# Induced attention and a squared-ReLU feed-forward: from lanes of 480 tokens to lanes of 512

## The chip, the core and the metric

One core of one Trainium2 chip runs the whole program. The metric is the time of one execution on the device, in microseconds (us). A core has TensorE (PE in the profile; its weight loads are PEld), VectorE (DVE), ScalarE (ACT), GpSimd (POOL) and SyncE (SP), which here issues nearly all DMA transfers. Each engine works through its own instructions in the order in which the program lists them, and semaphores hold it back until its operands are there.

## The reference

Four batches of 12480 tokens of 128 channels; 32 inducing vectors attend to each batch, and the batch attends to the result. A feed-forward layer of width 2048 follows on all 49920 tokens.

```python
def mab(q, kv):
    s = scale * (q @ kv.transpose(0, 2, 1))
    s = s - s.max(-1, keepdims=True)
    a = np.exp(s)
    a /= a.sum(-1, keepdims=True) + 1e-09
    return a @ kv
h = mab(I, x)
x = mab(x, h).reshape(49920, 128)

h = np.maximum(x @ w_in, 0.0)
return h * h @ w_out
```

Everything is float32.

## The kernel before

**Lanes, groups and blocks.** A lane is 480 tokens (NR = 15 rows of S = 32). Four lanes make a group, with the 32 inducing vectors of each lane on 32 of the 128 partitions. A batch has six groups of four lanes and a seventh of two. One lane is one block of the feed-forward layer, so there are 104 blocks.

**First attention** (`First`, L412, for batches 1 to 3; `FirstBatch`, L571, for batch 0). x is loaded a group at a time, turned so that channels lie on partitions (DVE turns 32x32 blocks at L452 and SP moves them at L462; batch 0 uses PE at L711), and multiplied with the inducing vectors (L481, four narrow fp32 products with 32 columns of the array each). The maximum of each lane is taken (L488). To have one maximum over the four lanes, DVE spreads the maxima into four columns (L492), PE adds up over partitions with the matrix `same` (L495), which writes into free columns of the same PSUM bank (480 to 483 of 512), and DVE takes the maximum (L499, L506). ACT takes the exponentials (L516), DVE turns them (L526), and PE mixes the tokens (L534, 15 steps). At the end of a batch, `first_end` (L758) normalises and joins the lanes to `hT`; then the product of h and w_in is made (`wide`, L793, four fp32 products of 512 columns a batch), rounded to fp32r by ACT (L797), and the remainder taken by DVE (L802). The result `hw` holds high and low parts and serves as the first weights of the batch.

**Second attention** (`Second`, L820): scores against `hT` (L836), softmax on DVE and ACT (L842 to L870), split into a high and a low fp32r part (L873, L877), and spread by SP to `st`, four transfers a lane (L883). The lanes of the short group are read as four lanes of 256 tokens that overlap, and the two blocks put together from them.

**Feed-forward** (`ffn_block`, L964): a block has four quads of four slices of the hidden width. A quad has four first products, `hw` with `st` in fp32r (L991); ReLU on ACT in two halves (L998); the square on ACT (L1013); rounding to fp32r on DVE (`hi`, L1018) and the remainder (`lo`, L1023); and three second products a slice: hi with wo_hi, hi with wo_lo, lo with wo_hi (L1077). In the last quad of a block the fourth slice is left unsplit and takes one fp32 product instead (`exact`, L1067, weights `wo_whole`). The first two blocks of all are wholly fp32 (`PLAIN`, L1034), as the split weights aren't ready then. DVE turns the output (L1098), and SP stores it (L1105).

**Weights** arrive as 64-bit words of which both halves are read, and are decoded by one ACT and five DVE instructions per 512 columns (`weights`, L283 to L327; joined at L369 and L388).

**The order** of every engine's instructions is written out by a planner before the program runs (`Plan`, L44). Each task has engines, an assumed duration in ns, a due time and predecessors; buffers have a number of places (`room`). `run` (L84) lists the tasks one after the other: for each engine, among those that can start, the one with the earliest due time. Due times come from the start of the block (BLOCK apart, from T_MAIN on) and the constants at L195 to L217. `narrow` (L1141) puts the parts of first and second attention that fall into a group's slot (mixing of the group before, scores, second attention's scores) into one stretch on PE, as a change between narrow and wide products costs PE time in the planner (L54, L67).

```python
narrow(due, parts, ...)                       # L1177: all parts of the slot in one task
t = add("DVE", 100, lanes, due + TOP_DUE, [t])                    # L556
t = add("PE", 110, gather, due + TOP_DUE, [t], reads=[bank_])     # L557
t = add("DVE", 100, most, due + TOP_DUE, [t], reads=[bank_])      # L558
exact = j == NQ - 1 and WHOLE(b, g, k) and not plain              # L980
```

Of the kernel before, what the change touches and what calls it, by code (L numbers as in the profile page):

```python
# [22 lines left out]
NR = 15  # L23
# [3 lines left out]
class Task:  # L27
    def __init__(self, engine, ns, fn, due, needs, port, mode, takes, late, order):
# [4 lines left out]
        self.waiting = 0  # L33
        self.then = []
# [9 lines left out]
class Plan:  # L44
# [12 lines left out]
    def __init__(self, room, begin, stick=0.0, patience=(0.0, 0.0, 40.0), waits={}, margin=0.0):  # L57

        self.room, self.begin, self.stick, self.tasks = room, begin, stick, []
        self.patience = patience
        self.waits, self.margin = waits, margin
# [20 lines left out]
    def run(self):  # L84
# [15 lines left out]
        for t in self.tasks:  # L100
            t.waiting = len(set(t.needs))
            for n in set(t.needs):
                n.then.append(t)
        for t in self.tasks:
            if not t.waiting:
                offer(t)

        def room_at(t):
            at = 0.0
            n = {}  # L110
            for b in t.takes:
# [3 lines left out]
                if i >= 0:  # L115
                    for u in (old[i].users if i < len(old) else ()):
                        if u.end is None:
# [4 lines left out]
        while len(done) < len(self.tasks):  # L122
            best = None
            for e in self.ENGINES:
                pick = None
                ways = []
                for t in open_[e]:
# [6 lines left out]
                    due = t.due - self.stick if e == "PE" and mode and t.mode and free[e] > self.begin else t.due  # L134
                    ways.append((start, due, t.order, t))
                if ways:
# [4 lines left out]
                    if e in self.waits and now > self.begin:  # L141
                        over = [w for w in ways if w[1] < f[1] - self.margin and f[0] < w[0] < f[0] + ns
                                and w[0] - f[0] < self.waits[e] * (f[0] + ns - w[0])]
# [5 lines left out]
            if best is None:  # L149
                raise RuntimeError("the plan is stuck")  # L150
# [22 lines left out]
def induced_attention_then_squared_relu_ffn(  # L173
# [15 lines left out]
    lanes_of = [Q] * (N // (Q * LANE)) + ([N % (Q * LANE) // LANE] if N % (Q * LANE) else [])  # L189
    NG = len(lanes_of)  # L190
    first_lane = [sum(lanes_of[:g]) for g in range(NG)]
    groups = [(b, g) for b in range(B) for g in range(NG)]
    scale = 1.0 / math.sqrt(C)

    GB, HB, LB, MB, STB, XTB, XNB, XBB = 3, 2, 2, 2, 6, 7, 2, 2  # L195
    T_MAIN, BLOCK = 41600.0, 10300.0
    ORDER = "x0 x1 x2 x3 i0 x4 x5 x6 i1 i2 i3 o0 o1 o2 o3".split()
    W_DUE = [20500.0, 27300.0, 31000.0, 32500.0, 43500.0, 42700.0, 47000.0, 53600.0]
    FIRST_DUE, FIRST_STEP, MIX_DUE, MIX_STEP, MINI_DUE = 5800.0, 3100.0, 22400.0, 200.0, -1000.0
    SLOT, SLOT_LAST, NARROW = 20300.0, -18700.0, 880.0  # L200
    AFTER = None
    WAIT_PE, WAIT_ACT, WAIT_DVE, MARGIN = 0.0, 0.9, 0.75, 10100.0
    LOAD_LEAD, TOP_DUE, GAIN_DUE, END_DUE = 29200.0, 6000.0, 3500.0, 23100.0
    S2_LEAD_0, S2_STEP, S1_LEAD, S1_STEP = 22200.0, 1400.0, 8700.0, 5600.0
    WHOLE = lambda b, g, k: True
# [5 lines left out]
    KEPT = 5  # L211
    SPLIT_DUE, SPLIT_STEP, PLAIN_DUE = 65000.0, 200.0, 6000.0
    FIRST_PAIRS, LAST_PAIRS = 2, 1
    G1_DUE, SQ_DUE, HI_DUE, LO_DUE, OP_DUE = -3000.0, 8100.0, 3100.0, 5000.0, 14500.0
    OT_DUE = 7300.0
# [4 lines left out]
    xn_pool = ctx.enter_context(tc.tile_pool(name="xn", bufs=XNB))  # L220
    xb_pool = ctx.enter_context(tc.tile_pool(name="xb", bufs=XBB))
# [9 lines left out]
    plan = Plan(dict(xn=XNB, early=5, tp=2, s=4, xb=XBB, xt=XTB, st=STB, m=MB, h=2, o0=1, o1=1, g=GB, hi=HB, lo=LB, sw=1, a=1, d=2, e=2, et=2), T_MAIN, patience=PATIENCE,  # L231
                waits={"PE": WAIT_PE, "ACT": WAIT_ACT, "DVE": WAIT_DVE}, margin=MARGIN)
# [8 lines left out]
    ind_sb = const.tile([M, C], F32, name="ind_sb")  # L241
# [12 lines left out]
    identr = const.tile([P, P], F32R, name="identr")  # L254
# [962 lines left out]
```

## Time and profile before

| | |
|---|---|
| median of 3 runs | 1621.41 us (1621.02 to 1621.56) |
| the profiled execution's own time | 1622.28 us |
| its span on the core | 1620.2 us |
| mean granted TensorE clock | 0.995 |
| busy: DVE, ACT | 1539.8 us, 1523.3 us |
| first products of the first block begin | 51.12 us |

The page gives busy times and shares of the span, 40 slices of the span in tenths, the chain of work that ended last (followed back from the last instruction, at each step to what released it) and groups of instructions by line and form: count, busy us, mean ns of one, idle time ahead of them and what ended it. A mean duration of a matmul includes its way through the array, which overlaps with the next one; how fast they follow each other is read from runs in the chain or from the starts in the timeline.

### The profile page before, as it was taken

Reading aid. Unit: us, or ns where it says so; the run is one execution under the profiler, and the core shown is the slowest. Engines: PE = TensorE matmul, PEld = TensorE weight load, DVE = VectorE, ACT = ScalarE, POOL = GpSimd, SP = SyncE. Lnnn points to the kernel's source line nnn. Section 1 sums busy time; section 2 is a strip of 40 time slices with the busy share of each in tenths; the row PEclk is TensorE's granted clock in tenths of the full one; section 3 lists DMA queues with packets and bytes.
Section 4 is the critical chain, followed back from the end, with each engine's and each line's share of the span. In section 5 each row is a group of like instructions: output and inputs, shape, how many; then the busy total and the mean of one; then the engine's idle time right before and its main releaser. Section 6 shows DMA issues by size and latency. Waiting matters only on the chain.

```text
span 1620.2 us, 22156 instructions
## 1 busy us (share of the span) xinstructions
PE 1599.4 (99%) x8006; PEld 1285.4 (79%) x8006; DVE 1539.8 (95%) x1471; ACT 1523.3 (94%) x1423; POOL 49.8 (3%) x39
## 2 busy tenths in 40 slices
PE   7899999999999999999999999999999999999998
PEld 5478888887778888888777888888878888888886
DVE  6789999999999999999999999999999999999997
ACT  5799999999999999999999999999999999999997
POOL 0000000000000000000000000000000000000000
PEclk9899999999999999999999999999999999999999
DMA  6431322422332233233332322422312211212211
GB/s 237 121 88 36 54 68 58 92 52 59 85 63 55 56 74 68 60 70 68 80 73 45 64 64 57 91 54 58 76 34 44 43 30 29 40 29 34 43 31 19
DMA packets 249308, 101.29 MB, mean 63 GB/s; under 512 B 219088, under 2 KB 245360, under 8 KB 249200
## 3 DMA queue, kind: packets, MB, share of 16 engines
q1 hardware_dynamic: 248240, 99.77, 27.7%
q8 instruction: 63, 1.03, 0.3%
q14 instruction: 45, 0.37, 0.1%
q10 hardware_dynamic: 960, 0.11, 0.0%
HBM read 29.77 MB, written 25.56 MB: 34 GB/s over the span
## 4 chain that ended last, share of the span: by engine, by line
PE 93%; DVE 3%; DMA 2%; issue 1%; ACT 1%; SPq 0%; DVEq 0%
PE op L1077 60%; PE h L991 22%; PE op L1067 5%; PE op L1034 2%; PE na L836 1%; PE nb L534 1%; DVE lo L1023 1%; PE sp L481 1%; DMA lo_i<-in_moe_w_in_dram 1%; PE wp L793 1%; DVE hi L1018 1%; DMA xn<-in_x_dram 1%; ACT g L998 0%; PE sp L495 0%; DVE et L642 0%
## 5 line engine op out<-in xcount | busy, mean ns | idle before, releaser
L1023 DVE TENSOR_TENSOR lo<-g,hi 128x1920 fp32r<-128x1920 f32 (+1 forms) x409 | 824.3, 2016 | 24.0 <-PE op L1077 5.1
L998 ACT ACTIVATE g<-h 128x960 f32<-128x960 f32 x832 | 779.5, 979 | 48.8 <-PE h L991 33.1
L1013 ACT ACTIVATE g<-g 128x1920 f32<-128x1920 f32 (+1 forms) x419 | 757.4, 1809 | 3.4
L991 PE MATMUL h<-st,hw 128*128 128x480 f32 x1664 | 521.8, 397 | 1.3 <-ACT g L998 1.3
L1018 DVE CAST hi<-g 128x1920 fp32r<-128x1920 f32 (+1 forms) x409 | 442.0, 1081 | 15.5 <-ACT g L1013 12.3
L1077 PE MATMUL op<-hi,wo_hi 128*128 128x480 f32 x1530 | 443.6, 396 | 0.0
L1077 PE MATMUL op<-lo,wo_hi 128*128 128x480 f32 x1530 | 434.2, 381 | 0.6 <-DVE lo L1023 0.5
L1077 PE MATMUL op<-hi,wo_lo 128*128 128x480 f32 x1530 | 415.6, 380 | 0.0
L991 PEld LDWEIGHTS h<-st,hw 128*128 128x128 f32 x1664 | 309.6, 188 | 93.5 <-issue 25.6
L1077 PEld LDWEIGHTS op<-hi,wo_hi 128*128 128x128 f32 x1530 | 285.8, 188 | 70.0 <-issue 25.2
L1077 PEld LDWEIGHTS op<-lo,wo_hi 128*128 128x128 f32 x1530 | 286.3, 188 | 51.2 <-DVE lo L1023 3.3
L1077 PEld LDWEIGHTS op<-hi,wo_lo 128*128 128x128 f32 x1530 | 286.7, 188 | 47.4 <-issue 0.8
L1067 PE MATMUL op<-g,wo_whole 128*128 128x480 f32 x204 | 98.9, 566 | 0.0
L860 POOL TENSOR_SCALAR z<-z 128x15 f32<-128x15 f32 (+1 forms) x28 | 48.7, 1739 | 1497.3 <-DVE z L856 1497.3
L1098 DVE STREAM_TRANSPOSE ob<-op 128x480 f32<-128x480 f32 (+1 forms) x105 | 70.4, 671 | 2.2 <-PE op L1077 1.9
L452 DVE STREAM_TRANSPOSE xb<-xn 128x960 f32<-128x960 f32 (+1 forms) x42 | 49.2, 1171 | 9.4 <-DMA xt<-xb 8.6
L1067 PEld LDWEIGHTS op<-g,wo_whole 128*128 128x128 f32 x204 | 38.2, 188 | 8.1 <-issue 2.4
L836 PE MATMUL na<-xt,hT 128*32 128x480 f32 (+1 forms) x224 | 29.7, 559 | 0.0
L481 PE MATMUL sp<-xt,indT 128*32 128x480 f32 x156 | 23.6, 570 | 0.0
L534 PE MATMUL nb<-xn,et 128*32 128x128 f32 (+1 forms) x630 | 22.5, 275 | 0.0
L534 PEld LDWEIGHTS nb<-xn,et 128*32 128x32 f32 (+1 forms) x630 | 16.9, 109 | 7.0 <-issue 5.7
L842 DVE STREAM_TRANSPOSE d<-na 128x480 f32<-128x480 f32 (+1 forms) x28 | 18.0, 641 | 3.0 <-PE na L836 3.0
(136 smaller groups left out, 471.1 us busy)
## 6 DMA issues: line engine op xcount, KB each, us to landing
out_dram<-ob SPq DMA_DIRECT2D x412, 60.0 KB, 2.2
xn<-in_x_dram SPq DMA_DIRECT2D x24, 960.0 KB, 5.5
st<-sw SPq DMA_DIRECT2D x380, 60.0 KB, 2.0
xt<-xb SPq DMA_DIRECT2D x312, 60.0 KB, 2.0
xn<-in_x_dram SPq DMA_DIRECT2D x4, 480.0 KB, 5.5
hi_i<-in_moe_w_in_dram SPq DMA_DIRECT2D x2, 512.0 KB, 14.7
lo_i<-in_moe_w_in_dram SPq DMA_DIRECT2D x2, 512.0 KB, 17.6
hi_o<-in_moe_w_out_dram SPq DMA_DIRECT2D x2, 512.0 KB, 5.0
```

The lines of the kernel that those rows point to most:

```text
L452: nc.vector.transpose(v["xb"][:R].rearrange("p j r t -> p r j t"), self.xn[:R, :, 2 * h * S:2 * (h + 1) * S].rearrange("p r (j c) -> p r j ...
L534: nc.tensor.matmul(v["nb"][c * M:(c + 1) * M, :], self.et[:R, r, :], self.xn[:R, r, :], start=r < Q, stop=r >= NR - Q,)
L836: nc.tensor.matmul(v["na"][i * M:(i + 1) * M, :W], s["hT"][:, :M], cols[:, c:c + W], start=True, stop=True,)
L860: E.tensor_scalar(v["z"], v["z"], 1e-9, 0.0, ALU.add, ALU.add)
L991: nc.tensor.matmul(c["hp"][:, l, :LANE], s["hw"][:, f * P:(f + 1) * P], second.st[k], start=True, stop=True,)
L998: nc.scalar.activation(v["g"][:, 2 * i:2 * i + 2, :], c["hp"][:, :, :LANE], AF.Relu)
L1013: nc.scalar.activation(v["g"][:, h], v["g"][:, h], AF.Square)
L1018: nc.vector.tensor_copy(v["hi"][:, h], v["g"][:, h])
L1023: nc.vector.tensor_sub(v["lo"][:, h], v["g"][:, h], v["hi"][:, h])
L1067: nc.tensor.matmul(w["op"][:, :LANE], wo_whole, v["g"][:, 3, :], start=False, stop=False)
L1077: nc.tensor.matmul(w["op"][:, :LANE], pools["wo"][wo][:, 4 * j + l, :], v[name][:, l, :], start=(j == x_ == 0 and l == 0), stop=(j == NQ - ...
L1098: nc.vector.transpose(w["ob"][:, rows].rearrange("p r c -> p (r c)"), w["op"][:, rows.start * S:rows.stop * S])
```

## The change

- **Lanes of 512.** NR is 16. A batch has six whole groups and 192 tokens left over, which form a seventh, small group of two lanes of 96 tokens in first attention and one lane of 192 in second. T_MAIN, BLOCK and the other constants of the planner are new.
- **A shared block.** The 192 tokens left over of batches 0 and 1 make one block of 384 tokens at the end of batch 0, those of 2 and 3 one at the end of batch 2. Its first products come in two halves, each with the weights of its batch. There are 96 blocks of 512 and two of 384.
- **Lane maxima by transfers.** For batches 1 to 3 the 512 scores fill the PSUM bank. `exchange` moves the maxima between partitions with SBUF-to-SBUF transfers on SP: seven for four lanes, five for two. `lanes` and `gather` go. Batch 0 keeps its gather, in a bank of its own, and is cut into parts of four and three groups instead of five and two.
- **First weights by one product.** For batches 1 to 3 the four products of `first_end` become one stretch of four narrow ones into one bank; one rounding and one remainder follow, and 16 transfers place them in `hw`.
- **Exact slices.** The number of exact slices a block depends on block and batch: quad 3 in three of four blocks, quads 1 and 3 in the fourth; in the last batch quad 3 in every second block and none in the others.
- **The planner.** `back` derives due times for the tasks ahead of the first block from what follows them. `reserve` plans the chain to the first block's `st`, `hw` and first output weights alone and then fixes its DVE and ACT tasks at those times. `GROUPED` makes each part of a slot a stretch of its own. PE gets filling products of 128 columns, 3 and 4 at the very start, 16 and 64 in gaps of the first stage, due behind everything else.
- **Smaller ones.** x of the first group loads in two pieces; `a` lies in `sw`; `identr` and `ind_sb` share a place; the seventh group's x lies in an `st` place.

```diff
-NR = 15
+NR = 16
@@ reserve
+        for t in self.run(chain):
+            if t.by in ("ACT", "DVE"):
+                t.ns = t.ns[t.engine.index(t.by)] if isinstance(t.ns, tuple) else t.ns
+                t.engine, t.at = [t.by], t.start
+            t.due = t.start - 1e5 if t.by != "SP" else t.due
@@ run
+                    if held[e] and t.at is None:
+                        ns = t.ns[t.engine.index(e)] if isinstance(t.ns, tuple) else t.ns
+                        if start + ns > max(held[e][0].at, held[e][0].ready or 0.0) + self.give:
+                            continue
...
+    lanes_of = [Q] * WHOLES + [2]
+    rows_of = [NR] * WHOLES + [3]
+    groups = [(b, g) for b in range(B) for g in range(WHOLES + 1 - b % 2)]
-    T_MAIN, BLOCK = 41600.0, 10300.0
+    T_MAIN, BLOCK = 36800.0, 11300.0
+    GROUPED = lambda parts: [[part] for part in parts]
+    GAP = 1600.0
-    WHOLE = lambda b, g, k: True
+    WHOLE = lambda b, g, k: ((3,), (3,), (3,), (1, 3))[k % 4] if b < 3 else ((3,), ())[k % 2]
+    PARTS = (0, 4, 7)
+    BUSY = (3, 4, 0, 16, 64)
+    def busy(t):
+        nc.tensor.matmul(t[:, :P], ident, ident, start=True, stop=True)
@@ First
-            def lanes():
-            def gather():
-                nc.tensor.matmul(v["sp"][:, LANE:LANE + L], same[:R, :], v["lanes"][:R, :L], start=True, stop=True)
+            def exchange():
                 v["lanes"] = tiny.tile([P, Q], F32, tag="lanes", name=f"lanes_{n}")
+                for k, q, q0, many in pieces:
+                    nc.sync.dma_start(
+                        v["lanes"][q * M:(q + many) * M, k:k + 1], v["mx"][q0 * M:(q0 + many) * M]
+                    )
...
+                t = add("SP", 620 * len(pieces), exchange, due + TOP_DUE, [t], late=0)
+                t = add("DVE", 100, most, due + MOST_DUE, [t])
@@ fill (new)
+            t = add("PE", 120, lambda i=i: fn(i), due + i, needs if i == 0 else [first],
+                    takes=[] if i else [b], reads=[b] if i else [])
@@ first_end, later batches
+            for i, k in enumerate(ks):
+                nc.tensor.matmul(
+                    v["wp"][i * M:(i + 1) * M, :], s["hT"][:, :M], w_in_sb[:, k * WCH:(k + 1) * WCH], start=True, stop=True,
+                )
...
+            for a in range(4):
+                nc.sync.dma_start(
+                    s["hw"][a * M:(a + 1) * M, k * WCH:(k + 1) * WCH].bitcast(F32),
+                    v["wa"][i * M:(i + 1) * M, a // 2].bitcast(F32),
+                )
@@ ffn_block
-            exact = j == NQ - 1 and WHOLE(b, g, k) and not plain
+            exact = j in WHOLE(b, g, k) and not plain
+                    for c_, c0, c1 in spans:
+                        nc.tensor.matmul(
+                            c["hp"][:, l, c0:c1], state[c_]["hw"][:, f * P:(f + 1) * P], second.st[k][:, c0:c1],
+                            start=True, stop=True,
+                        )
@@ main
-            narrow(due, parts, AFTER and g < NG - 1 and made[AFTER[0]]["wide", AFTER[1]] or None)
+        for i, group in enumerate(GROUPED(parts)):
+            narrow(due + GAP * i, group)
```

More of the change, by code (lines that the diff above doesn't have):

```diff
@@ L82, in add, with back, visit, reserve @@
         return t
-    def run(self):
+    def back(self, tasks):
+        some, seen = set(map(id, tasks)), set()
+        def visit(t):
+            if id(t) in seen or id(t) not in some:
+                return
+            seen.add(id(t))
+            for n in t.next:
+                visit(n)
+            ns = max(t.ns) if isinstance(t.ns, tuple) else t.ns
+            lag = min(self.LATENCY[e] for e in t.engine)
+            t.due = min((n.due - (0.0 if n.engine == t.engine and t.engine[0] in ("PE", "SP") else lag) for n in t.next), default=self.begin) - ns
+        for t in tasks:
+            visit(t)
+    def reserve(self, chain):
+        for t in self.run(chain):
[3 more added lines that the diff above has]
+            t.due = t.start - 1e5 if t.by != "SP" else t.due
+    def run(self, tasks=None):
+        tasks = self.tasks if tasks is None else tasks
+        some = set(map(id, tasks))
+        for t in tasks:
+            t.start = t.end = None
+            t.then = []
+        held = {e: sorted((t for t in tasks if t.at is not None and t.engine == [e]), key=lambda t: t.at) for e in self.ENGINES}
         free = {e: 0.0 for e in self.ENGINES}
@@ L149, in run @@
             if best is None:
-                raise RuntimeError("the plan is stuck")
+                if not any(held.values()):
+                    raise RuntimeError("the plan is stuck")
+                held = {e: [] for e in held}
+                continue
             _, start, t, e = best
@@ new lines, in first_end @@
+        if b == 0:
+            for k in ks:
+                bw = Buffer("m" if k else "h")
+                d = due + 2 * step + k * step
+                t = w_gate[f"w0_{k}"] = add("PE", 870, lambda k=k: wide(k), d, [s["joined"], w_ins[k]] + opened, takes=[bw])
+                t = w_gate[f"p0_{k}"] = add("ACT", 520, lambda k=k: part(k), d, [t], reads=[bw])
+                s["wide"].append(add("DVE", 725, lambda k=k: rest(k), d, [t], reads=[bw]))
+            return
+        R = M * len(ks)
@@ new lines, in place_wide @@
+        def place_wide(i, k):
+            for a in range(4):
[3 more added lines that the diff above has]
+                )
+        bw, ba = Buffer("m"), Buffer("xb")
+        d = due + 2 * step + WIDE_DUE
+        t = add("PE", 1010, lanes, d, [s["joined"]] + [w_ins[k] for k in ks] + opened, mode="n", takes=[bw])
+        th2 = add("ACT|DVE", (560, 600), high, d + 1000, [t], takes=[ba], reads=[bw])
@@ L1082, in quad @@
                 begin = j == x_ == 0
-                last = add("PE", 219 if exact and i else 438, products, due + OP_DUE - ahead + 600 * x_,
+                last = add("PE", pass_ns(W) * (2 - (exact and i)), products, due + OP_DUE - ahead + 600 * x_,
                            [from_[min(i, len(from_) - 1)], last, w_split],
@@ L1184, in induced_attention_then_squared_relu_ffn @@
+    plan.back([t for t in plan.tasks[:first_tasks] if t.engine != ["SP"] and t.due < 1e6])
+    chain = set()
+    for level in LEVELS(mini.ready[0], state[0]["wide"], [v[2] for v in w_outs]):
+        ends = list(level)
+        while ends:
+            t = ends.pop()
+            if t not in chain:
+                chain.add(t)
+                ends += t.needs
+        plan.reserve([t for t in plan.tasks if t in chain])
     for t in plan.run():
```

490 lines of the change are left out of this document (288 added, 202 removed).

## The prediction

> **What bounds the kernel now.** I read the page first (busy shares and the chain that ended last), then the windows of the span, then the groups by form, and last the chain of waits in order of time.
>
> ```profile
> PE 1599.4 (99%) x8006; PEld 1285.4 (79%) x8006; DVE 1539.8 (95%) x1471; ACT 1523.3 (94%) x1423; POOL 49.8 (3%) x39
> ...
> PE 93%; DVE 3%; DMA 2%; issue 1%; ACT 1%; SPq 0%; DVEq 0%
> ```
>
> TensorE is busy for 99% of the span and owns 93% of the chain. VectorE and ScalarE are close behind, so the share alone settles nothing; the windows do.
>
> ```profile
> 30.00:40.00 10.00, 8.03 (x215) 6.49 (x216) 9.96 (x29) 5.00 (x14) 0.00 (x0) 1.00 0.19 57
> 40.00:50.00 10.00, 7.34 (x26) 2.73 (x26) 9.43 (x26) 2.60 (x5) 0.00 (x0) 0.51 0.66 225
> 50.00:60.00 10.00, 8.35 (x22) 4.43 (x20) 8.86 (x18) 8.01 (x11) 0.68 (x1) 0.81 0.19 78
> ...
> 400.00:800.00 400.00, 399.75 (x2036) 323.68 (x2035) 392.05 (x370) 382.68 (x355) 13.05 (x8) 1.00 0.30 66
> ```
>
> Columns: window, length, then busy time of PE, PEld, DVE, ACT and POOL, granted clock, DMA share, GB/s. In steady state PE is busy for 399.75 of 400 us, DVE for 392.05 (98%), ACT for 382.68. So every PE microsecond taken out shortens the run, as long as DVE follows. From 30 to 60 us it is DVE that is full (28.25 of 30 us), while PE's clock is at 0.51 and 0.81.
>
> A busy PE is only a bound if its instructions run at their own pace. The chain gives that pace:
>
> ```profile
> 62.18 4.03 PE op L1034 x10
> ...
> 270.00 2.40 PE op L1077 x11
> ```
>
> ```profile
> 423.85 0.94 PE na L836 x8
> ...
> 425.65 1.72 PE wp L793 x4
> ```
>
> An fp32r pass of 480 columns (L1077; L991's are of the same type and shape, and I take the same for them) takes 2.40/11 = 0.2185 us. An fp32 product is two records; at 480 columns one takes 4.03/10 = 0.403 us (0.806 a product), at 512 columns 1.72/4 = 0.430 us. So 32 more columns cost 0.027 us for the two passes of a record, 0.0134 us a pass.
>
> ```profile
> L991 PE MATMUL h<-st,hw 128*128 128x480 f32 x1664 | 521.8, 397 | 1.3 <-ACT g L998 1.3
> L1077 PE MATMUL op<-hi,wo_hi 128*128 128x480 f32 x1530 | 443.6, 396 | 0.0
> L1077 PE MATMUL op<-lo,wo_hi 128*128 128x480 f32 x1530 | 434.2, 381 | 0.6 <-DVE lo L1023 0.5
> L1077 PE MATMUL op<-hi,wo_lo 128*128 128x480 f32 x1530 | 415.6, 380 | 0.0
> ```
>
> The counts are x1664 and three times x1530, with under 2 us of idle time ahead of them all. Hence my sum: PE's instructions before and after, each at its pace.
>
> **The main products.** Before: 1664 + 4590 = 6254 passes x 0.2185 = 1366.5 us, and 102 exact products (L1067) plus 32 plain ones (L1034, two blocks of 16), 134 x 0.806 = 108.0. Together 1474.5 us.
>
> After: 96 blocks of 512 tokens and two of 384. WHOLE gives one exact product to 64 of the 512-token blocks (16 + 45 passes), two to 18 (58 passes), none to 12 (64 passes); two stay plain (16 passes and 16 products). That is 3904 + 1044 + 768 + 32 = 5748 passes. I take 0.2185 + 0.0134 = 0.2319 us each: 1333.0. The low end is no growth, 0.2185 (77 us less), if the weight load and not the columns set the pace; the high end is in proportion, 0.2331 (6.9 us more). The row that tells about the load:
>
> ```profile
> 23.53 1.62 PE L711 MATMUL xtp<-ident,xn 128*128 128x128 f32 x15
> ```
>
> 15 products with a 128x128 load each, in 0.108 us apiece: a load does not need 0.2185 us, so the low end drops out, and the fp32 rows, which differ in nothing but columns, decide. The Trainium skill (TensorE: Matmul & The Clock Gate, Back-to-back issue gap) gives N/2.4 + 2.5 ns, an estimate of 202.5 ns at 480 columns; the trace has 218.5 ns, and the measurement decides. By the page the pass at 512 would be 215.8 ns, the change of these products about +2 us, and the sum below some 6 us later.
>
> The 100 exact and 32 plain products of 512 columns: 264 records x 0.430 = 113.5. The two shared blocks: 64 first products of 192 columns (between 0.108, the row above, and 0.2185; I take 0.11, as columns set the pace; the high end adds 7 us), 90 passes of 384 at 0.178, two exact products: 7.0 + 16.0 + 1.3. Sum 1470.8, so **-3.7 us**. Fewer passes and their fixed part are the gain; more exact products give some of it back.
>
> **The narrow products.** Joined, in one stretch:
>
> ```profile
> 257.23 0.90 PE nb L534 x27
> 258.12 0.09 PE sp L481
> 258.21 0.01 PE nb L534 x2
> 258.23 0.80 PE sp L481 x7
> 259.03 0.81 PE na L836 x8
> ```
>
> Second attention's scores cost 0.81 us here and 0.94 alone (the row at 423.85): a stretch of its own costs 0.13 more. The gather that goes:
>
> ```profile
> 272.68 0.28 PE L495 MATMUL sp<-lanes,same_m 128*128 128x4 f32 x2
> 272.82 0.68 PE L1077 MATMUL op<-hi,wo_hi 128*128 128x480 f32 x2
> 273.34 0.59 PE L1077 MATMUL op<-hi,wo_lo 128*128 128x480 f32 x2
> ```
>
> It takes 0.14 us, and the two passes behind it 0.52 instead of 0.44: 0.22 in all. Terms: 21 gathers gone, -4.6. Three later batches' first weights: four products of 0.86 become one narrow stretch like the scores, 1.00 us, 3 x (3.44 - 1.00) = -7.3. For the 18 whole groups of batches 1 to 3 and the 23 score stretches of the second attention, 32 more columns at 0.055, and a sixteenth mixing step at 0.06: +3.3. The rest groups, with 96 tokens a lane where there were 480: mixing had as many products as in a whole group, so that I take 0.91 + 0.89 = 1.8 us from the rows above for mixing and scores; now a fifth of it and two stretches, about 0.7. Three times that, and the second attention's a little: -3.5. GROUPED gives each part a stretch of its own: 0 to 36 more stretches x 0.13 = 0 to +4.7; the due times lie 1.6 us apart, about seven passes, so I take 27: +3.5. Sum **-8.6**.
>
> **The start.** DVE carries it, so what is moved there is judged by the chain:
>
> ```profile
> 32.40 0.48 DVE lo_i L324
> ...
> 46.56 0.33 DVE lo_o L306
> ...
> 48.46 3.65 PE wp L793 x4
> ...
> 58.19 1.04 PE op L1034 x2
> ```
>
> Between 32.40 and 46.89 us 17 pieces of weight decoding, first and last above, stand in the chain with 6.7 us; then four records of `wp` at half clock, 3.65 us, two products that only later quads need. Only from 58.19 us on does PE run through. reserve() places the first block's chain ahead of all this. At best 6.7 + 3.65 = 10.4 us go; but decoding doesn't vanish, it comes due later, and DVE has only 1.75 us free in 30 to 60 us. The clock is the other part: 7.34 x 0.49 + 8.35 x 0.19 = 5.2 us of PE time went to it. Against that stand 80 filling products of 128 columns, two records of 0.403 x 128/480 each, 0.215 us where the plan says 0.12: 17.2 us; cover is PE's idle time of 30 to 60 us (6.3) with those 5.2, and some 4 us could come out on the path. Ends -10.4 and +4; no row is nearer to either, so the middle with the clock's part counted: **-5**. At the end of the run the last block has no exact product; its extra quarter of casting on DVE costs **+1**.
>
> Sum: -3.7 - 8.6 - 5 + 1 = -16.3. The profiled execution took 1622.3 us (span 1620.2 and 2.1 around it), 0.9 over the median of the runs; against the median 1621.4 - 16.3 = **1605.1 us**.
>
> **Does DVE follow?**
>
> ```profile
> L1023 DVE TENSOR_TENSOR lo<-g,hi 128x1920 fp32r<-128x1920 f32 x306 | 656.5, 2145 | 18.5 <-PE op L1077 4.8 <-DVE hi L1018 0.5 <-PE h L991 0.5
> L1018 DVE CAST hi<-g 128x1920 fp32r<-128x1920 f32 x306 | 350.1, 1144 | 14.4 <-ACT g L1013 11.3 <-PE op L1077 2.3
> L1023 DVE TENSOR_TENSOR lo<-g,hi 128x1440 fp32r<-128x1440 f32 x101 | 166.1, 1644 | 5.5 <-PE op L1077 0.3
> L1018 DVE CAST hi<-g 128x1440 fp32r<-128x1440 f32 x101 | 90.9, 900 | 1.1 <-ACT g L1013 1.0
> ```
>
> Four blocks now: 12 x (1.144 + 2.145) + 4 x (0.900 + 1.644) = 49.6 us, and 98% of PE's 59.4 leaves 8.6 for the rest. After, along the slope of these rows: 11 x 3.49 + 5 x 2.69 = 51.8, with 9.1 for the rest 60.9, against 63.2 on PE: 96%. Slack 2.3 us a group. In the last batch, without first attention but with fewer exact products, 98%. So DVE follows, unless it is made to wait.
>
> **The rivals.**
>
> First, a wait takes the gather's place, and the kernel gets slower. The maxima go over SP as seven transfers, and `most` stands in DVE's queue behind them; behind `most` are the casts that PE lives on.
>
> ```profile
> 400.66 10.12 SPq L883 DMA_DIRECT2D st<-sw  x14
> ```
>
> ```profile
> st<-sw SPq DMA_DIRECT2D x380, 60.0 KB, 2.0
> ```
>
> Seven issues at 10.12/14 = 0.72 us and 2.0 to land make 7 us, more if such a run of 14 is in front. If DVE stood still for a wait w each time, the loss over 18 groups is 18 x (w - 2.3) us; it passes the gain and 0.2% from w = 3.4 on, and with w = 5 the time is 1605 + 49 = 1654 us. Against it: `most` is an own task, and DVE has some 16 casts a group to do meanwhile; mixing only follows in the next group, 63 us on. The Trainium skill (DMA: Bandwidth & Descriptors, Specifications) says that transfers under 512 B a piece are read-modify-write; these pieces are 4 B, and no run here shows such. 8%.
>
> Second, hand-over between batches: the weights now go out in 16 transfers, 16 x 0.72 + 2 = 13.5 us more on the way to the next batch, three times. If none is hidden, +40: 1645 us. Against it: the chain from the last group's scores on has 7 us for the maxima, these 13.5, 4 x 0.72 + 2 = 4.9 for `st` and, an estimate, some 10 us of short steps, 35 us in all, and the 63 us of that group to hide in. 3%.
>
> Third, the clock. The page on TensorE named above (Part 1) lets the clock fall after an idle window of about 3.4 us. Here it falls at 40 us, though in 30 to 40 us PE was idle for 1.97 us in all: the trace disagrees. What the rows allow as a mechanism is that the filling doesn't keep the clock up; then the start gives nothing: 1610 us. 20%.
>
> Fourth, the change doesn't make PE shorter than by a trifle: passes in proportion to columns (+6.9), all stretches apart (+1.2), a start without gain (+5): 1618 us. 12%.
>
> **How the numbers follow.** The forecast has 57%, with its own range 1596 to 1613. The third rival is faster too. The fourth lies on the edge of 0.2% (3.2 us, about what a measurement of this kernel can tell from no change): half each. Faster 0.57 + 0.20 + 0.06 = 0.83, same 0.06, slower 0.11. The range reaches from 1595 (start at its best, -5.4, and no stretch apart, -3.5, with rounding up) to 1618 (the fourth rival); it leaves out the first two rivals.
>
> **What would show it.** Right: L991 and L1077 at about 0.232 us a pass in the chain, PE busy in steady state as now, `h` and the plain products some 5 us earlier, clock 1.0 through 40 to 55 us, L495 gone. Wrong: a DVE wait on a DMA ahead of `top`, PE idle ahead of the first `h` of a batch, a pass far from 0.232, or DVE at 100% with PE waiting for `lo`.

## The result and the profile after

The kernel after took 1637.98 us (median of 4 runs, 1637.14 to 1639.25), the kernel before beside it 1621.22 us (1620.48 to 1621.56). The ratio is 1.0102, with a 95% interval of 1.0088 to 1.0116: slower by 1%, where 1605.1 was forecast. The page of after, busy times and the chain by engine:

```profile
PE 1619.4 (99%) x7714; PEld 1214.2 (74%) x7714; DVE 1531.4 (94%) x1392; ACT 1517.0 (93%) x1338; POOL 41.5 (3%) x39
...
PE 96%; DMA 1%; DVE 1%; SPq 1%; ACT 1%; issue 0%; DVEq 0%; ACTq 0%
```

TensorE still owns the chain, and its busy time has grown by 20 us, though it has 292 instructions fewer. (The filling products count as busy.) The windows that answer to those of before, with the same columns:

```profile
30.00:40.00 10.00, 9.00 (x197) 7.71 (x196) 9.29 (x25) 4.94 (x14) 0.00 (x0) 1.00 0.02 4
40.00:50.00 10.00, 9.54 (x78) 7.55 (x79) 6.54 (x19) 0.95 (x3) 0.00 (x0) 1.00 0.15 46
50.00:60.00 10.00, 10.00 (x79) 9.21 (x78) 8.77 (x18) 6.21 (x9) 0.64 (x1) 1.00 0.72 266
400.00:800.00 400.00, 396.10 (x1872) 295.82 (x1871) 379.45 (x339) 373.46 (x328) 4.49 (x7) 0.99 0.31 68
```

The clock is at 1.00 throughout the start, as forecast, but VectorE has 3.65 us less work in these 30 us than before (24.60 against 28.25): it stands idle where before it was nearly full. From 400 to 800 us TensorE misses 3.90 us, where before it missed 0.25.

To see where the time goes, I add up from the timeline of TensorE the columns of all products that write `h` and `op` (each record of an fp32 product counted twice) and note when the product begins with which a given share is reached. Time behind the kernel before at the same share, in us:

| share of the products | before at | after | e13 | e14 | e15 | e16 | e18 |
|---|---|---|---|---|---|---|---|
| 0 (first `h`) | 51.12 | +1.4 | +1.6 | +1.9 | +1.7 | +2.0 | +1.5 |
| 12% | 239.02 | +13.7 | +13.3 | +6.0 | +10.5 | +3.4 | +8.4 |
| 24% | 432.44 | +9.2 | +8.8 | +1.6 | +6.3 | -1.1 | +4.2 |
| 28% | 496.34 | +18.3 | +10.1 | +2.8 | +7.1 | -0.2 | +5.0 |
| 100% | 1614.68 | +17.2 | +7.9 | +0.6 | +1.1 | -5.6 | -1.1 |

(e13 to e18 are runs of the next section; plain, exact and narrow products lie at other places in each kernel, so a few microseconds within a column say nothing.) After loses 14 us by 12%, mostly behind the first `h`, and 9.1 between 24% and 28%, where batch 0 gives way to batch 1. (The expectations below have 8.8 for it, from a coarser count.) In the remaining 72% it gains 1.1, where my sum without the start, -11.3, would have given 8.1.

The first hand-over in the queue of SP, which issues the transfers (start, us, line, tiles, count):

```profile
419.55 2.52 SPq L1034 DMA_DIRECT2D st_pair<-sw  x4
...
450.32 14.80 SPq L578 DMA_DIRECT2D lanes<-mx  x12
465.21 2.62 SPq L1278 DMA_DIRECT2D out_dram<-ob  x4
467.94 10.73 SPq L1034 DMA_DIRECT2D st<-sw  x16
```

and what TensorE, VectorE and ScalarE waited for between 440 and 500 us (total, times, longest):

```profile
PE h L1154 <- ACT g L1162: 3.0, 4, 2.0
...
DVE sw L1017 <- DMA st<-sw: 3.3, 1, 3.3
...
ACT e L601 <- DVE neg L591: 4.9, 1, 4.9
```

TensorE's waits, the 3.9 us missing above, are less than half of the 9.1. Most of the rest is its clock, which falls behind them (windows with the columns of before):

```profile
478.00:480.00 2.00, 0.79 (x3) 0.30 (x2) 0.00 (x0) 2.00 (x3) 0.00 (x0) 1.00 0.40 98
480.00:482.00 2.00, 0.93 (x2) 0.30 (x2) 1.73 (x3) 2.00 (x4) 0.00 (x0) 0.84 0.14 20
482.00:484.00 2.00, 1.40 (x3) 1.16 (x4) 1.97 (x2) 2.00 (x2) 0.00 (x0) 0.50 0.15 21
...
486.00:488.00 2.00, 2.00 (x6) 1.52 (x6) 1.97 (x2) 1.79 (x1) 0.00 (x0) 0.50 0.13 19
```

The 14 passes that start from 482.60 us on take 5.89 us, where 0.233 us each (the pace below) would make 3.26: another 2.6 us, though no single wait was longer than 2.0.

`sw` of batch 1's first group was complete at 429.1 us (the low part at 428.4, 0.69 us long). Its 16 transfers go out 39 us later, and the next turn into `sw` on VectorE waits for the last of them, casts behind it. In before the first four of these transfers left as soon as the parts were there, the other twelve behind four stores:

```profile
437.06 5.20 SPq L883 DMA_DIRECT2D st<-sw  x4
...
445.01 7.59 SPq L883 DMA_DIRECT2D st<-sw  x12
```

### The profile page after: what moved, and what is told of

It is laid out like the page before. It is cut to its first block, busy times and chain, and to the rows that moved or that the text cites. A ratio compares the mean times of both kernels' runs of the same rounds, so it can differ in the third digit from the quotient of the medians.

```text
span 1637.4 us, 21466 instructions
## 1 busy us (share of the span) xinstructions
PE 1619.4 (99%) x7714; PEld 1214.2 (74%) x7714; DVE 1531.4 (94%) x1392; ACT 1517.0 (93%) x1338; POOL 41.5 (3%) x39
## 4 chain that ended last, share of the span: by engine, by line
PE 96%; DMA 1%; DVE 1%; SPq 1%; ACT 1%; issue 0%; DVEq 0%; ACTq 0%
PE op L1241 61%; PE h L1154 22%; PE op L1231 5%; PE op L1198 2%; PE na L982 2%; PE sp L558 1%; PE nb L621 1%; DMA xn<-in_x_dram 1%; PE idle_o L321 1%; ACT g L1162 0%; SPq L1034 0%; SPq L539 0%; DMA xt<-xb 0%; SPq L799 0%; PE wp L902 0%
## 5 line engine op out<-in xcount | busy, mean ns | idle before, releaser
L1187 DVE TENSOR_TENSOR lo<-g,hi 128x2048 fp32r<-128x2048 f32 (+2 forms) x385 | 817.9, 2124 | 25.9 <-PE op L1241 6.9
L1162 ACT ACTIVATE g<-h 128x1024 f32<-128x1024 f32 (+1 forms) x784 | 776.2, 1034 | 58.3 <-PE h L1154 40.7
L1177 ACT ACTIVATE g<-g 128x2048 f32<-128x2048 f32 (+2 forms) x395 | 755.6, 1913 | 4.7
L1154 PE MATMUL h<-st,hw 128*128 128x512 f32 x1536 | 510.2, 414 | 3.8 <-ACT g L1162 3.4
L1182 DVE CAST hi<-g 128x2048 fp32r<-128x2048 f32 (+2 forms) x385 | 437.3, 1136 | 33.7 <-PE op L1241 13.2
L1241 PE MATMUL op<-hi,wo_hi 128*128 128x512 f32 (+1 forms) x1434 | 433.4, 410 | 0.7 <-DVE hi L1182 0.7
L1241 PE MATMUL op<-lo,wo_hi 128*128 128x512 f32 (+1 forms) x1434 | 419.4, 395 | 0.0
L1241 PE MATMUL op<-hi,wo_lo 128*128 128x512 f32 (+1 forms) x1434 | 418.2, 395 | 0.0
L1231 PE MATMUL op<-g,wo_whole 128*128 128x512 f32 (+1 forms) x204 | 103.7, 590 | 0.0
L1267 DVE STREAM_TRANSPOSE ob<-op 128x512 f32<-128x512 f32 (+2 forms) x99 | 69.3, 700 | 3.6 <-PE op L1241 3.0
## 6 DMA issues: line engine op xcount, KB each, us to landing
hi_i<-in_moe_w_in_dram SPq DMA_DIRECT2D x2, 512.0 KB, 13.7
```

Of the source, the lines that this page charges most:

```text
L1154: nc.tensor.matmul(c["hp"][:, l, c0:c1], state[c_]["hw"][:, f * P:(f + 1) * P], second.st[k][:, c0:c1], start=True, stop=True,)
L1162: nc.scalar.activation(v["g"][:, 2 * i:2 * i + 2, :W], c["hp"][:, :, :W], AF.Relu)
L1177: nc.scalar.activation(v["g"][:, h, :W], v["g"][:, h, :W], AF.Square)
L1182: nc.vector.tensor_copy(v["hi"][:, h, :W], v["g"][:, h, :W])
L1187: nc.vector.tensor_sub(v["lo"][:, h, :W], v["g"][:, h, :W], v["hi"][:, h, :W])
L1231: nc.tensor.matmul(w["op"][:, :W], wo_whole[:, KEPT_F.index(j)], v["g"][:, 3, :W], start=False, stop=False)
```

## The experiments

Each kernel ran beside the kernel before; ratios are to it, with their 95% intervals. The first four took the parts that I suspected first.

**e1, filling products silent** (planned, not issued).

```diff
-            busy(v["t"])
+            pass
```

> The changed kernel with the 80 filling products of the first stage planned as before but not issued; every other instruction keeps its place on its engine. Theory A (a filling product takes 0.22 us where the plan has 0.12, and the real work stands behind it in PE's queue): the first block's h and the first plain products come 5 to 9 us earlier than in the changed kernel (first h from 52.5 to about 46 us), and the time falls by 5 to 9 us, to 1629 to 1633. Rival (the decoding on DVE sets the start whatever PE does): under 2 us. A third way: without them the clock falls to half in the start, which takes back 3 to 5 us of the gain.

1636.94 us, 1.0092 (1.0077 to 1.0107). The clock of the start falls without them, and the time is that of after within the intervals:

```profile
40.00:50.00 10.00, 8.52 (x69) 3.70 (x60) 6.04 (x20) 0.90 (x2) 0.00 (x0) 0.50 0.01 2
50.00:60.00 10.00, 8.47 (x16) 4.76 (x17) 9.49 (x19) 6.83 (x10) 0.64 (x1) 0.50 0.75 274
```

The filling does keep the clock at 1.00, but filling and clock together are worth nothing here: without them the first `h` comes 0.5 us later, and at 12% the kernel is 1.4 us further on. Theory A falls. That a gain by the clock and the filling's own time cancel isn't ruled out.

**e2, own maximum.** The transfers between lanes are left out and each lane uses its own maximum (the first attention of batches 1 to 3 is not the reference's); the order of the rest stays.

```diff
-                    nc.sync.dma_start(
-                        v["lanes"][q * M:(q + many) * M, k:k + 1], v["mx"][q0 * M:(q0 + many) * M]
-                    )
...
+                nc.vector.tensor_reduce(v["top"][:R], v["mx"][:R], axis=AX.X, op=ALU.max)
```

> The changed kernel with the transfers of the lane maxima left out: each lane uses its own maximum, so the softmax of the first attention of batches 1 to 3 is not the reference's. Every engine's order is that of the changed kernel (three memsets more on DVE). Theory B (the transfers block SP's queue and make ACT wait for the shift, and so PE stops at the hand-over after the shared block): PE's idle time at 473 to 483 us and the half clock behind it go, and the other hand-overs gain a little: 8 to 13 us, to 1625 to 1630. Rival (the stop lies in the order itself, with the shared block's smaller quads and three places for g): under 3 us.

1636.79 us, 1.0092 (1.0077 to 1.0107). Without a transfer, ScalarE's wait for `neg` is 4.9 us as before and VectorE's for `st<-sw` 2.9. Theory B falls: the stop at the hand-over is written into the order, and the transfers of the exchange don't cause it.

**e3, all parts of a slot in one stretch.**

```diff
-    GROUPED = lambda parts: [[part] for part in parts]
+    GROUPED = lambda parts: [parts] if parts else []
```

> The changed kernel with the parts of a slot in one stretch on PE again; the order is planned anew. Theory C (each separate narrow stretch costs PE 0.3 us: 0.13 in itself and 0.19 in the products behind it): 36 stretches fewer, 7 to 11 us less, 1627 to 1631. Rival (the stretches were apart in time only where PE had room): under 3 us, or slower, as a long stretch of 2.7 us holds up the products that ACT and DVE wait for.

1662.16 us, 1.0251 (1.0234 to 1.0268). The first hand-over alone holds TensorE for 18.5 us (mixing waits for `et`) and 6.9 us (`h` waits for `st<-sw`), and 41 us are lost by 28%. From there to the end it gains 1.3. Joining everything makes the hand-over worse before it can show what a stretch costs.

**e4, the kernel before with the one product for the later batches' first weights** (the lines of `first_end` in the diff, put into before).

> The kernel before with one part of the change: first weights of batches 1 to 3 by one narrow stretch, one rounding, one remainder and 16 transfers each. By PE's sum 3 x (3.44 - 1.0) = 7 us less: 1614. Rival (hand-over: the weights come 10 us later over SP, and PE waits for them at three batch starts): slower than 1621 by up to 20 us.

1623.35 us, 1.0012 (1.0003 to 1.0022). Busy time of TensorE falls from 1599.4 to 1596.5 us, 2.9 us where the sum has 7.3, and at the first hand-over new waits come:

```profile
PE h L1026 <- ACT g L1033: 2.2, 3, 1.9
PE op L1112 <- DVE lo L1058: 1.0, 1, 1.0
```

At the last hand-over it waits another 2.5 us. By itself this part brings nothing.

**e5, no held chain, and e10, no derived due times.**

```diff
-    LEVELS = lambda st, hw, wo: [[st, hw[0], wo[0]]]
+    LEVELS = lambda st, hw, wo: []
...
-    plan.back([t for t in plan.tasks[:first_tasks] if t.engine != ["SP"] and t.due < 1e6])
```

(the first line in e5, the second in e10)

> No task is fixed ahead of the others in the first stage; everything else is as after. Theory A: fixing the first block's chain keeps weight decoding off VectorE while VectorE stands idle (9.29 us busy of 30-40, 6.54 of 40-50, where before had 9.96 and 9.43), so the first plain product comes at 61.91 instead of 58.19. Then without it the first plain product comes at about 58 to 59, the first stage loses 2 to 4 us against before instead of 11 to 15, and the time is about 1628 to 1631. Theory B: the new due times of the weights set that order, whatever is fixed: first plain product at 61 to 63, time 1635 to 1640.

> Due times ahead of the first block stay as written, not derived backwards from what follows; the chain is still fixed ahead. Theory G: the derived due times put the decoding of w_in and w_out behind the chain, so that the third and fourth piece are joined at 56.46 and 62.62 and lo_o at 69.85 us (before: 39.62, 43.01 and 54.07); without them the first stage loses about 4 instead of 11 us by 4% of the products: 1629 to 1632. Rival: the constants order the decoding late as well: 1635 or more.

1652.00 us, 1.0186 (1.0170 to 1.0201), and 1652.03 us, 1.0188 (1.0173 to 1.0204). Theories A and G fall: at 12% they are 13.3 and 13.6 us behind before, as after is. (Without the held chain the first `h` comes 6.1 us later than in after, and at 12% nothing is left of that.) The further loss comes around the first hand-over (at 24% already +27.1 and +26.8), where TensorE waits 8.9 us for `et` in both. So a total time said nothing on the start as long as the hand-over stood in it.

**e6, a place of its own for `a`** (one of those of `e`), instead of lying in `sw`.

```diff
-                v["a"] = v["sw"][:RW, 1, :W].bitcast(F32)
+                a = att.tile([P, NR, S], F32, tag="e", name=f"a_{n}")
+                v["a"] = a.rearrange("p r t -> p (r t)")[:RW, :W]
```

> The second attention's weights, turned back, get a place of their own (one of the two that hold first attention's exponentials) instead of lying in sw, as after has it. Theory C: at the first hand-over between batches VectorE stands 3.34 us in the turn into sw, because the last st<-sw transfers still read that place; casts are queued behind it, and TensorE waits. Then with the place of its own this wait goes, and of the 8.8 us that the first hand-over loses 3 to 6 go: 1632 to 1635. Rival: the cast into sw right behind the turn waits for the same transfers instead, and nothing moves: 1636 to 1640.

1640.57 us, 1.0118 (1.0103 to 1.0134). Theory C falls; the wait moves to the cast behind the turn, as the rival said (3.0 us for `st<-sw`).

**e7, the gather back on TensorE** for all batches.

```diff
-                t = add("SP", 620 * len(pieces), exchange, due + TOP_DUE, [t], late=0)
-                t = add("DVE", 100, most, due + MOST_DUE, [t])
+                t = add("DVE", 100, lanes, due + TOP_DUE, [t])
+                t = add("PE", 110, gather, due + TOP_DUE, [t], **({"takes": [bg]} if self.whole else {"reads": [bg]}))
+                t = add("DVE", 100, most, due + MOST_DUE, [t], reads=[bg])
```

> The lane maxima of the later batches are spread and gathered by a product on TensorE as before, into a bank of its own (the short group's into free columns of its scores' bank); no transfers, and the order is planned anew. Theory D: the exchange (12 transfers that hold SP's queue for 14.80 us at 450 us, with st<-sw behind them) is what makes the first hand-over late: ScalarE's wait of 4.90 us for neg and VectorE's of 3.34 us for st<-sw go, 6 to 9 us less, and 21 gathers of 0.14 to 0.22 us come back, +3 to +4.6: 1632 to 1636. Rival: the hand-over is late because casts, exponentials and turns of several groups fall together there, whatever moves the maxima: the waits stay and the gathers are added: 1639 to 1643.

1649.32 us, 1.0175 (1.0158 to 1.0192). The first hand-over stays (28%: +17.9), so theory D falls, and the second one now loses 13 us as well (44%: +22.4, 48%: +35.1). Why it does wasn't followed up (the gather needs a bank of its own in PSUM); the exchange is the better way in this plan.

**e8, before's start in after**: before's due times and constants for the first stage and the weights, parts of five and two groups, no held chain, no derived due times, no filling.

```diff
-    T_MAIN, BLOCK = 36800.0, 11300.0
+    T_MAIN, BLOCK = 41600.0, 11300.0
...
-    PARTS = (0, 4, 7)
-    KEPT = 6
+    PARTS = (0, 5, 7)
+    KEPT = 5
...
-    BUSY = (3, 4, 0, 16, 64)
+    BUSY = (0, 0, 0, 0, 0)
```

> After, with the due times of before for the first stage and the weights, two parts of five and two groups, nothing fixed ahead and no filling products. Theory E: the loss of 11 to 15 us by 4 to 8% of the products is the new order of the first stage: first plain product back at about 58 to 59 and the time about 1624 to 1628. Rival: it comes from what the wider lanes do there (a group of 512 columns is turned, scored and kept more slowly, one more exact weight slice): first plain product still at 61 or later, 1634 or more.

1632.74 us, 1.0068 (1.0053 to 1.0083). At 12% it is 8.3 us behind instead of 13.7, at 28% 12.5: the start was worth about 5 to 6 us, the hand-over was left. The time lies between theory E's (1624 to 1628) and the rival's.

**e9, the slot of a batch's first group one block later; e11, the maximum of that group free of the short group's; e12, e8 with e11.**

```diff
-        due = starts[b, g] + (SLOT if g < WHOLES - 1 else SLOT_LAST)
+        due = starts[b, g] + (SLOT + 11300.0 * (g == 0 < b) if g < WHOLES - 1 else SLOT_LAST)
...
-                t = add("DVE", wide_ns(W), top, due + TOP_DUE, [t, back("shifted")], reads=[bank_])
+                t = add("DVE", wide_ns(W), top, due + TOP_DUE, [t, None if self.g == 0 and self.b > 1 else back("shifted")], reads=[bank_])
...
-                t = add("DVE", 100, most, due + MOST_DUE, [t])
+                t = add("DVE", 100, most, due + MOST_DUE, [t, back("shifted")])
```

(the first pair of lines is e9, the others are e11)

> The slot of each later batch's first group (scores of two groups of the next batch's first attention, and the scores of the second group) comes one block later; the order is otherwise planned as after, the same up to 440 us. Theory F: this slot falls together with the change from batch 0 to batch 1 behind the shared block of only 384 tokens (VectorE's turns, sums and products between 470 and 478 us in place of casts), and that crowd is what the first hand-over's 8.8 us are. Then they go for the most part: 1630 to 1633. Rival: the new batch's own chain is late, wherever the slot lies: 1636 to 1640.

> The lane maxima of a later batch's first whole group are taken without waiting for the short group's final maximum (that final maximum is still waited for one step later); only the instructions around 440 to 490 us, and the same place of the next batch, change their order. Theory H: the maximum taken 10 us after its scores (460.14 against 449.4) holds SP's queue for 7.3 us, ScalarE's exponentials for 4.90 us, and st<-sw behind them; without it ScalarE's wait is under 1 us, VectorE's wait for st<-sw goes, and of the 8.8 us of the first hand-over 5 to 8 go: 1630 to 1633. Rival: those queues are late anyway, and the time stays within 2 us of after: 1636 to 1640.

> The run with before's start (1632.7) and the free maximum together. Theory H: the two gains add up, as they lie at different places: 1625 to 1628. Rival: the hand-over stays: 1631 to 1634. Neither theory gives less than before's 1621.

1649.01 us, 1.0169 (1.0154 to 1.0184); 1642.71 us, 1.0130 (1.0113 to 1.0147); 1636.60 us, 1.0093 (1.0078 to 1.0108). All three are slower than the kernel that they start from. Theories F and H fall, but e11 gave the hint: the maxima were early, and VectorE's wait for the transfers of `st` grew.

```profile
DVE sw L1017 <- DMA st<-sw: 8.9, 1, 8.9
```

In e11 these transfers left at 472.23, in e9 at 476.44, whatever came earlier. They had been ready for over 40 us. What were they waiting for? Not for data, so for a place: `st` has six, which the plan gives out in turn. In after the x of batch 2's small group sits in that ring. It is loaded as soon as SP is free (one of the two loads at 306.91; the other is a whole group's), and its place comes free when it has been mixed, behind 469.25 us:

```profile
306.91 0.98 SPq L504 DMA_DIRECT2D xn<-in_x_dram  x2
```

```profile
469.25 0.68 PE nb L621 x8
```

Six takings later stands the first `st` of batch 1. So the planner lists its transfers behind the mixing, and SP, which issues in the order listed, gets to them only behind the exchange and four stores. (On the chip the first of them left 1.3 us ahead of the mixing: by then the order held them back, not the place.) The x of batch 3's small group does the same at the second hand-over: twelve of the 16 transfers leave at 869.50 us, behind its mixing at 865.44. But the first four had left at 827.04, and TensorE waits for nothing there.

**e13, an own place for the small group's x.** `d` gives up one of its two places for the room; with that alone the plan's order stays that of after, instruction by instruction.

```diff
-                    t = st_pool.tile([P, LANE], F32R, tag="st", name=f"xn_{self.n}").bitcast(F32)
-                    self.xn = t[:, :self.NR * C].rearrange("p (r c) -> p r c", c=C)
+                    self.xn = att.tile([P, self.NR, C], F32, tag="xr", name=f"xn_{self.n}", bufs=1)
...
```

> The small group's x gets a place of its own instead of one in the ring of st (d has one place instead of two to make room; that alone leaves the order of after as it is). Theory I: the x of a later batch's small group takes a place of st some 40 us before it is needed and holds it until it is mixed at 469 us; the ring gives places in turn, so the next batch's first st<-sw, ready at 428.9 us, waits behind it until 467.94, and with it sw, VectorE and ScalarE. Then st<-sw starts at about 430 us, no PE wait of over 0.5 us stands between 450 and 500 us, and 6 to 9 us go: 1629 to 1632. Rival: the crowd of VectorE's work at the hand-over stays: 1636 to 1640.

1630.08 us, 1.0048 (1.0033 to 1.0063): 7.9 us less than after. The queue of SP in the same stretch:

```profile
427.66 10.43 SPq L1033 DMA_DIRECT2D st<-sw  x16
...
449.92 15.02 SPq L577 DMA_DIRECT2D lanes<-mx  x12
```

The transfers leave 40 us earlier; between 440 and 500 us TensorE waits for nothing, and ScalarE's wait for `neg` is 0.3 us, with the exchange as long as it was. The clock stays at 1.00 as well. Of the 9.1 us lost between 24% and 28%, 1.3 are left. Theory I holds.

**e14, e15, e16: own place with before's start; own place with the scores of a slot joined; all three.**

```diff
-    GROUPED = lambda parts: [[part] for part in parts]
+    GROUPED = lambda parts: [parts[:1], parts[1:]] if len(parts) > 2 else [parts] if parts else []
```

> The own place together with before's start (1632.7 alone). Theory I: the two add up: 1624 to 1627. Rival: 1631 to 1634.

> The own place, and the scores of first and second attention of a slot in one stretch on TensorE again, mixing apart. Theory J: a separate stretch costs 0.13 us and the product behind it 0.19 us more, so that some 20 joined stretches give 3 to 6 us on top of the own place: 1624 to 1628. Rival: as with all three in one stretch, joining makes later steps late and the gain is eaten: 1629 or more.

> Own place, before's start and the scores joined. If the three losses are what lies between the kernels, the time is 1618 to 1623, at before's 1621.4, and wider lanes give nothing by themselves, as the pass grows with its columns. Rival: something else is lost in the steady state as well, and the time stays at 1625 or more; or the wider lanes do gain, and it falls below 1617.

1623.62 us, 1.0008 (0.9999 to 1.0017); 1622.96 us, 1.0005 (0.9996 to 1.0015); 1617.03 us, 0.9970 (0.9959 to 0.9981). The losses add up: the own place 7.9, the start 6.5, the joined scores 7.1, each to within some 2 us by the intervals, together 21.5 of the 1637.98, which leaves 1616.5; all three at once give 1617.0. e16 beats both kernels, and its time lies below the 1618 to 1623 expected for it: wider lanes do give something by themselves, 5.0 us.

**e17, e16 with after's due times of the weights; e18, e16 with after's held chain, derived due times and filling.**

```diff
-    W_DUE = [20500.0, 27300.0, 31000.0, 32500.0, 43500.0, 42700.0, 47000.0, 53600.0]
+    W_DUE = [20700.0, 29500.0, 40000.0, 33500.0, 42900.0, 42900.0, 46000.0, 48100.0]
...
-    LEVELS = lambda st, hw, wo: []
+    LEVELS = lambda st, hw, wo: [[st, hw[0], wo[0]]]
```

(the first pair of lines is e17, which also takes after's SPLIT_DUE, SPLIT_STEP and PLAIN_DUE; the second is e18, which also takes after's call of `back` and its BUSY)

> The fastest run so far (1617.0: own place, before's start, scores joined), but with after's due times for decoding the weights and splitting them. Theory K: these due times make the output weights late (lo_o joined at 69.85 in after, 54.07 in before), and most of the 6 us come back: 1621 to 1624. Rival: they don't matter by themselves: 1616 to 1619.

> The fastest run so far, but with after's holding of the first block's chain, the derived due times and the filling products, on before's constants. Theory L: fixing that chain first pushes weight decoding behind it, and the output weights come late: 1621 to 1624. Rival: holding is harmless or brings the first block forward: 1613 to 1618.

1617.49 us, 0.9979 (0.9970 to 0.9988), and 1622.69 us, 1.0004 (0.9994 to 1.0013). Theory K falls, L holds: the due times of the weights don't matter by themselves; e18 takes 5.2 us more than e17 beside it and 5.7 more than e16. What the held chain does is seen on VectorE, where a piece of the output weights, `lo_o`, is joined (start, us, line, tiles) in e18

```profile
67.38 0.69 DVE L454 TENSOR_TENSOR lo_o<-lo_o 128x512 f32<-128x512 f32 x1
```

and in e16

```profile
55.73 0.63 DVE L454 TENSOR_TENSOR lo_o<-lo_o 128x512 f32<-128x512 f32 x1
```

In after this row stands at 69.85, and TensorE waits for it; in before at 54.07:

```profile
70.56 3.70 PE L1198 MATMUL op<-g,lo_o 128*128 128x512 f32 x8 [1.26 <-DVE lo_o L454]
```

The first `h` comes only 0.6 us earlier for it (52.61 in e18, 53.17 in e16), and the first plain product 5 us later:

```profile
57.70 1.10 PE L1197 MATMUL op<-g,hi_o 128*128 128x512 f32 x2 [1.51 <-DVE hi_o L454]
```

```profile
62.65 1.02 PE L1197 MATMUL op<-g,hi_o 128*128 128x512 f32 x2
```

(e16 and e18; 58.19 in before, 61.91 in after.) Of the three things in e18 the filling was harmless in e1. Taking away the holding alone (e5) or the derived due times alone (e10) left the loss at 12% as it was, so which of the two does the harm stays open.

## Why the prediction was wrong

The mechanism on which it rested, that each TensorE microsecond counts while VectorE follows, was right: VectorE stands at 379.45 us beside TensorE's 396.10, 96% as worked out, and away from the first hand-over TensorE's waits from 500 us on come to 0.4 us. The sum missed by 32.9 us, at these steps:

**The start, "-5": 11.5 us off.** "The middle with the clock's part counted" failed. It priced the clock, though e1 at half the clock and without the filling is no slower, and took the weight decoding that is moved back for hidden. The text itself said that "decoding doesn't vanish, it comes due later"; what it missed is that the first plain products live on it: they begin 3.7 us later than before, not 5 earlier. (When the first one begins isn't all: in e10 it begins 1.3 us earlier than before, at 56.86 us, but TensorE then waits 1.0 us for `hw`, 0.8 for `lo_o` and 0.6 for `hi_o`, with filling products in between, and is 13.6 us behind at 12% all the same.) With the chain held, VectorE has 9.29 and 6.54 us of work where before had 9.96 and 9.43, and what it leaves undone there is missing later: TensorE waits for `lo_o` up to 70.56 us. The held chain with its company cost 6.5 us (e14 against e13; 5.7 in e18 against e16), and without it the start gained nothing of the 5 either (e16 at 12%: +3.4).

**The hand-over, at nothing: 7.9 us off.** The diff's line "the seventh group's x lies in an `st` place" was named among the smaller ones and not costed. Its cost lay in how long that place is held: some 160 us, of a ring given out in turn. The second rival had the right place and the wrong wait: the 16 transfers of `hw` left at 404.97 us, long before they were needed, and it was the 16 of `st` that came late, at a cost at one of three hand-overs. No term stood for the fallen clock behind such a wait either, 2.6 of these microseconds.

**The pass, "0.2319": 8.0 us off.** The fp32 slope was to carry over, with a fixed part that wider lanes save. The chain of after gives, for 512 columns:

```profile
270.85 2.33 PE op L1241 x10
...
1622.95 9.35 PE op L1241 x40
```

0.233 us a pass, also at the very end (0.2338), where VectorE and ScalarE have nothing left to do for it. For 384 columns in the shared block, from starts (four passes each):

```profile
462.61 0.88 PE L1241 MATMUL op<-hi,wo_hi 128*128 128x384 f32 x4
463.33 0.86 PE L1241 MATMUL op<-hi,wo_lo 128*128 128x384 f32 x4
464.02 0.86 PE L1241 MATMUL op<-lo,wo_hi 128*128 128x384 f32 x4
464.72 0.51 PE L1241 MATMUL op<-hi,wo_hi 128*128 128x384 f32 x2
```

2.11 us for 12 passes from 462.61 to the next start at 464.72, 0.176 us apiece. Per column that is 0.458 ns at 384, 0.455 at 480 and 0.456 at 512: in proportion, with no fixed part. The fp32 records were in proportion too, but at 0.84 ns a column for two passes, 0.42 a pass (0.403 us at 480, 0.430 at 512), so their slope was too small for fp32r. 5748 passes x 0.0014 = 8.0 us (2.40/11 is 0.2182, not 0.2185, which moves both sums by nearly the same); the bound named in the text (0.2331) was the truth, and so this part of the fourth rival. The rule that the Trainium skill (TensorE: Matmul & The Clock Gate, Back-to-back issue gap) gives for the gap of an isolated product makes 215.8 ns at 512, an estimate; the 233 of the trace are 8% more, as at 480.

**The separate stretches, "+3.5": at least 3.6 us off.** Joining the scores alone again gave 7.1 us (e15 against e13) and 6.6 (e16 against e14). The chain of after and that of e15:

```profile
302.13 0.47 PE h L1154 x2
...
306.33 0.99 PE sp L558 x8
307.33 0.66 PE h L1154 x2
...
317.90 0.99 PE na L982 x8
318.90 0.66 PE h L1154 x2
```

```profile
648.38 0.99 PE sp L557 x8
649.38 0.86 PE na L981 x8
650.24 0.67 PE op L1240 x2
```

Alone, `na` takes 0.99 us, behind `sp` 0.86: the 0.13 that I had. But the first passes behind a stretch take 0.66 instead of 0.47, once a stretch, 0.19 more. I had seen something like it behind the gather (0.52 instead of 0.44 for two passes), and booked it to the gather alone. The joining takes one stretch out of 18 slots: 18 x (0.13 + 0.19) = 5.8 us, near what was measured; the order was planned anew as well, and what that gave isn't known apart.

These are 31.0 of the 32.9 us; 1.9 stay open. What the change is worth without its three losses, 1617.0 against before's 1622.0 in the same runs, is 5.0 us; my terms with these steps put right (-16.3 + 8.0 for the pass, + 5 for the start, - 3.5 for the stretches) give a gain of 6.8.

Of the rivals, the first, given 8% for its sign, was not the mechanism: VectorE waited 1.2 us for the exchange in the whole run. The third is refuted by the clock of 1.00. The DVE check came out as said; the +1 for the end of the run wasn't measured by itself.

## What to carry over

When a buffer is put into a ring that others use, cost the time that it is held, not its size: the first taker one round later waits for it, in a queue that nobody connects with it, and the wait shows up three engines further on. Putting a critical chain first is paid by what stood beside it; look for who needs that next. And find the place of a loss by progress through the work, not by the total: several of the runs above looked like a verdict on the start and were one on the hand-over.

## What the hardware showed

An fp32r pass with a new 128x128 weight load goes at 0.455 to 0.458 ns a column from 384 to 512 columns. At 192 columns it takes 0.42/4 = 0.105 us, 0.55 ns a column:

```profile
451.55 0.42 PE h L1154 x4
```

A change between products of 32 and of 128 columns of the array costs 0.13 us on the way in and 0.19 on the way out. A clock of 0.50 followed waits of TensorE of 3.9 us in all within 9 us, the longest 2.0 (after, 473 to 482 us), and was back at 1.00 by 490 us. A clock of 0.68, 0.83 and 0.83 in the three windows of the start (e16) goes with a start that is 10 us ahead of one at 1.00 (after) at 12% of the products:

```profile
30.00:40.00 10.00, 8.77 (x200) 7.57 (x200) 8.82 (x23) 5.95 (x16) 0.00 (x0) 0.68 0.17 55
40.00:50.00 10.00, 5.60 (x29) 1.89 (x26) 9.73 (x30) 1.70 (x4) 0.00 (x0) 0.83 0.53 154
50.00:60.00 10.00, 8.12 (x21) 4.19 (x21) 9.81 (x20) 7.87 (x12) 0.37 (x2) 0.83 0.42 173
```

VectorE is busy there for 28.36 of 30 us, in after for 24.60.
